# A retuned issue plan for an attention and gated-MLP kernel: new plan table, out-projection gates, earlier tile loads and 24 more dummy matmuls

## The chip, the core and the metric

The kernel runs on one core of a Trainium2 chip. The metric is device time in microseconds (us) of one execution, taken as the median of several runs; lower is better. A profile is one execution of its own, with its own time.

## What is computed

One token block of 2048 x 640 goes through a layernorm without weights. The result `xn` feeds two branches: full softmax attention with 32 heads of 20 columns and an out-projection, and a gated MLP with 1728 hidden columns whose output goes through silu. The two are multiplied and added to the input.

```python
def _A_ref(x, wqkv, wo):                       # x: [1, 2048, 640], H = 32, Dh = 20
    qkv = (x @ wqkv).reshape(B, S, 3, H, Dh).transpose(2, 0, 3, 1, 4)
    q, k, v = qkv[0], qkv[1], qkv[2]
    p = _softmax(jnp.einsum("bhqd,bhkd->bhqk", q, k) * Dh ** -0.5, axis=-1)
    o = jnp.einsum("bhqk,bhkd->bhqd", p, v)
    return o.transpose(0, 2, 1, 3).reshape(B, S, D) @ wo

def _B_ref(x, w_gate, w_up, w_down):           # F = 1728
    h = _sigmoid(x @ w_gate) * (x @ w_up)
    return h @ w_down

xn = _layernorm(A_x)
return A_x + _A_ref(xn, A_wqkv, A_wo) * _silu(_B_ref(xn, B_w_gate, B_w_up, B_w_down))
```

## The kernel before

**Stages.** A prologue (the list `PRO`, written out by hand) loads the 16 token tiles, normalizes and transposes them into `xnT`, and makes the first keys, values and queries. `s_warm` and `s_tr` put dummy 128x128 matmuls (`dummies`, line 318) between its TensorE (PE) steps. `s_k` makes the four key chunks; the maximum of the keys (`s_km`, `s_mdp`, `s_md`) gives a bound that one matmul, `s_bound`, subtracts from the scores of the first query; `s_qe0` moves that query to SBUF. Then the first scores can start.

The main part walks over 32 blocks, each of four heads and 512 queries. A block has 64 score tiles of 128 keys x 512 queries. A score matmul uses 32 rows of the PE array (L928). A score tile is turned into exponentials in one of two ways: ScalarE (ACT) applies Exp (L142, `pt`), or VectorE (DVE) makes it by integer arithmetic: one pass per tile from PSUM (`iv`, L1305) and three passes per group of four tiles in SBUF (`pb`, L1016, L1019, L1022). Both feed the PV matmuls (L964), which use 21 columns of the array; four of them, one for each head, run side by side.

**PSUM.** `scA` is two slots of two banks each, filled by turns. One turn is called a slot here: PE writes two score tiles into `scA`, often a third for ACT or one or two for DVE into the four single banks `bk`; ACT then takes the two-bank tile (128x1024) and, where there is one, the third tile (128x512). PE can only refill a slot when ACT has read it. The four `bk` banks also hold the PV sum of the block, and the results of all other matmuls.

**The other work** is cut into items that fill PE between the scores: key, query and value projections, GLU matmuls (L704, L716), the down projection (L742) with its tanh on ACT, and, late, the out-projection (`mk_out`, matmuls L802; `mk_part`, matmuls L835, for the last 512 queries). An out-projection item has a PE step, then a DVE step `ev`: it multiplies the PSUM tile by the stored MLP output (`otmp`, L809), and POOL (or DVE, at the end) adds the input tile (L812). `load_out` (L778) loads both operands of a token tile, the input rows (L783) and the MLP rows `gq_dram` (L784), into memory that `xnT` no longer needs; two token tiles alternate, so a load waits until the tile two before has been used and stored. It is called when the first half of a tile starts on PE.

**What sets the order.** The order of PE, ACT and DVE is fixed when the program is built: a planner steps a model clock (`now`) in 0.01 us, keeps when each engine, bank and buffer comes free, and writes the next instruction for a free engine. At run time each engine goes through its list in order and waits where an operand isn't ready. The planner's choices depend on eighteen numbers (`RULE`, L38), which are replaced at the start of each block by a row of `PLAN` (L41): how long to hold PE for a score slot, how many tiles DVE may take, how many ready PV tiles open a bank (`held`), and so on. An item opens when its `pre` events are past in the model; a step of it can have `gates` as well. POOL and the DMA queue of SyncE (SP) are not in the planner: a scheduler orders them.

**Normalization.** At the end of a block DVE copies the PV sum (`norm_a`, L978), its row of sums goes through DRAM (`ld`, `lt`), DVE takes the reciprocal `rt` (`norm_b`, L988, in the model 6.5 us after the copy), which goes through DRAM once more (`rd`, `rl`), and POOL multiplies (`norm_c`, L1001). For the last block but one the result `o6` goes straight to SBUF (L1005). The last block uses a short chain on the engines (`chain`, L1080): ACT copies the sum (L1061), PE transposes, DVE divides (`rq`, L772, and `onq`), PE transposes back, ACT copies (L1078), and `tail_steps` closes with the last out-projection matmuls (L1052, L1056), DVE multiplies (L1098, L1105) and adds, and four stores.

Of the kernel before, what the change touches and what calls it, by code (L numbers as in the profile page):

```python
# [18 lines left out]
P = 128  # L19
# [19 lines left out]
            dmax=2, third=2, dord=0, mord=0, mfew=2, npv=4, held=48, burst=1, excl=1)  # L39
KEYS = tuple(RULE)  # L40
PLAN = (  # L41
    (0.25, 5, 0.15, 0.2, 0.5, 0, 0.4, 1, 0.0, 2, 2, 0, 0, 2, 4, 48, 1, 1),
    (0.25, 5, 0.15, 0.2, 0.5, 0, 0.4, 1, 0.0, 2, 1, 0, 3, 2, 4, 48, 1, 1),
    (0.25, 4, 0.15, 0.2, 0.8, 0.2, 0.4, 1, 8.0, 2, 2, 0, 0, 2, 4, 48, 1, 1),
    (0.25, 4, 0.15, 0, 0.8, 0.2, 0.4, 1, 0.0, 2, 2, 0, 0, 2, 4, 48, 0, 1),
    (0.25, 4, 0.15, 0, 0.8, 0.2, 0.4, 1, 0.0, 2, 2, 3, 0, 2, 4, 48, 0, 0),
    (0.2, 4, 0.15, 0.2, 0.2, 0.2, 0.4, 1, 0.0, 2, 2, 0, 0, 1, 4, 32, 1, 1),
    (0.25, 4, 0.15, 0.5, 0.8, 0.2, 0.4, 1, 0.0, 2, 2, 0, 0, 2, 4, 48, 1, 1),
    (0.25, 4, 0.3, 0.2, 0.35, 0.2, 0.4, 1, 0.0, 2, 2, 0, 0, 1, 4, 48, 1, 1),
    (0.25, 4, 0.3, 0.2, 0.35, 0.8, 0.4, 1, 0.0, 2, 2, 0, 0, 1, 4, 48, 1, 1),  # L50
    (0.3, 4, 0.3, 0.2, 0.35, 0.8, 0.4, 1, -2.0, 2, 2, 0, 0, 1, 4, 48, 1, 1),
    (0.3, 4, 0.3, 0.2, 0.35, 0.8, 0.4, 1, -2.0, 2, 2, 0, 0, 1, 4, 48, 1, 1),
    (0.25, 4, 0.15, 0.2, 0.2, 0.2, 0.4, 1, 0.0, 2, 2, 0, 0, 2, 4, 48, 0, 1),
    (0.2, 4, 0.15, 0.2, 0.2, 0.2, 0.2, 1, 0.0, 2, 2, 0, 0, 2, 4, 48, 0, 1),
    (0.25, 4, 0.15, 0.2, 0.2, 0.2, 0.4, 1, 0.0, 2, 0, 0, 0, 1, 4, 48, 0, 1),
    (0.25, 4, 0, 0.2, 0.2, 0.2, 0.4, 1, 0.0, 2, 0, 0, 0, 1, 4, 48, 1, 1),
    (0.25, 4, 0, 0, 0.2, 0.2, 0.4, 1, 4.0, 2, 0, 0, 0, 1, 4, 48, 1, 1),
    (0.3, 4, 0.15, 0.2, 0.2, 0.2, 0.4, 1, 0.0, 2, 2, 0, 0, 2, 4, 48, 1, 1),
    (0.3, 4, 0.15, 0.2, 0.2, 0.5, 0.7, 1, 0.0, 2, 2, 0, 0, 2, 4, 48, 1, 1),
    (0.25, 4, 0.15, 0.2, 0.2, 1.2, 0.4, 1, 0.0, 2, 2, 0, 0, 2, 4, 48, 1, 1),  # L60
    (0.25, 4, 0.15, 0.2, 0, 1.2, 0.4, 1, 0.0, 2, 2, 0, 0, 2, 4, 48, 1, 1),
    (0.25, 4, 0.3, 0.2, 0, 1.2, 0.4, 1, 0.0, 2, 2, 0, 0, 1, 4, 48, 1, 1),
    (0.25, 4, 0.3, 0.2, 0.5, 1.2, 0.4, 1, 0.0, 2, 1, 0, 0, 1, 4, 48, 1, 1),
    (0.25, 4, 0, 0.2, 0.8, 1.2, 0.4, 1, 0.0, 2, 2, 0, 0, 2, 4, 48, 1, 1),
    (0.25, 4, 0.15, 0.2, 0.2, 0.5, 0.4, 1, 0.0, 2, 1, 0, 0, 2, 4, 48, 1, 1),
    (0.45, 4, 0.15, 0.2, 0.2, 0.5, 0.4, 1, 0.0, 2, 1, 2, 0, 2, 4, 52, 1, 1),
    (0.25, 4, 0.15, 0.2, 0.2, 0.2, 0.4, 1, 0.0, 2, 1, 0, 0, 2, 4, 48, 1, 1),
    (0.25, 4, 0.15, 0.2, 0.2, 0.5, 0.4, 1, 0.0, 2, 1, 0, 0, 2, 4, 48, 1, 1),
    (0.25, 4, 0.15, 0.5, 0.2, 1.2, 0.4, 1, 0.0, 2, 2, 0, 2, 2, 4, 48, 1, 1),
    (0.25, 4, 0.15, 0.2, 0.35, 0.2, 0.4, 1, 0.0, 2, 2, 0, 0, 2, 4, 48, 1, 1),  # L70
    (0.25, 4, 0.15, 0.2, 0.2, 0.2, 0.4, 1, 0.0, 2, 0, 0, 0, 2, 4, 48, 1, 1),
    (0.25, 4, 0.15, 0.2, 0.35, 0.8, 0.4, 1, 14.0, 2, 1, 0, 0, 2, 4, 48, 1, 1),
    (0.25, 4, 0.15, 0.2, 0.2, 0.2, 0.4, 1, 0.0, 2, 2, 0, 0, 2, 4, 48, 1, 1),
)

PRO = (
# [35 lines left out]
def kernel(  # L112
# [146 lines left out]
    with tc.tile_pool(name="ln", bufs=2) as lp, \  # L259
# [105 lines left out]
        def s_k(eng, c):  # L365
            pks[c] = psP.tile([P, 512], FP32, tag="pk", bufs=1, name="psk")
            k_mm(pks[c], 0, c)

        def s_km(eng, c):
            maxed.append(c)  # L370
# [29 lines left out]

        def s_bound(eng):
            q_bound(pq[0], 0, pq[1])

        def s_qe0(eng):
            q_evac(pq[0], qts[0])
# [104 lines left out]
    def mk_k(g, c, at):  # L510
        st = {}

        def alloc():
            st["ps"] = misc_ps()
        mms = [lambda kd=kd: k_mm1(st["ps"], g, c, kd) for kd in range(KD)]
        return Item([("PE", alloc, [(T_MM, f) for f in mms]),
                     ("DVE", 0.66, lambda: k_evac(st["ps"], g, c), "free"),
                     ("DVE", 0.60, lambda: k_max(g, c), "", lambda t: mds_done(g, t))], at)

    def mds_done(g, t):  # L520
        if len(mk_n[g]) == NQC:
# [45 lines left out]
    def mk_ku(u, c, at):  # L567
        st = {}

        def alloc():  # L570
            st["ps"] = misc_ps()

        def ev():
            st["k"] = wk.tile([P, QC], BF16, tag="ku", bufs=2, name="ku")[0:UC, :]
            nc.vector.tensor_copy(out=st["k"], in_=st["ps"][0:UC, :])
            nc.sync.dma_start(out=kD[u][:, c * QC:(c + 1) * QC], in_=st["k"])

        def mx():
            if u not in mku:
                mku[u] = [wk.tile([UC, NQC], FP32, tag="mk4", bufs=2, name="mk4"), 0, None]  # L580
            nc.vector.tensor_reduce(out=mku[u][0][:, c:c + 1], in_=st["k"], axis=AXISX, op=ALU.max,
                                    apply_absolute_value=True)
            mku[u][1] += 1
            if mku[u][1] == NQC:
                mk = wk.tile([UC, 1], FP32, tag="mk", bufs=2, name="mk")
                nc.vector.tensor_reduce(out=mk, in_=mku[u][0], axis=AXISX, op=ALU.max)
                mku[u][2] = wk.tile([UC, UH], BF16, tag="mdu", bufs=2, name="mdu")
                nc.vector.tensor_scalar_mul(out=mku[u][2], in0=esum_u[0:UC, :], scalar1=mk[:, 0:1])

        def end(t):  # L590
            if mku[u][1] == NQC:
                ev_at[("mdu", u)] = t + 0.3
        return Item([("PE", alloc, [(T_MM, lambda kd=kd: u_mm(st, u, 1, c, kd)) for kd in range(KD)]),
                     ("DVE", 0.60, ev, "free", mark("kD", u, c)), ("DVE", 0.60, mx, "", end)], at,
                    pre=[("wu", u)])

    aqs = {}
# [180 lines left out]
    def load_out(tt):  # L778
# [3 lines left out]
        out_tiles[tt] = (o2[:, 0:D], o2[:, D:3 * D].bitcast(FP32))  # L782
        nc.sync.dma_start(out=out_tiles[tt][0], in_=x2[tt * P:(tt + 1) * P, :])  # L783
        nc.sync.dma_start(out=out_tiles[tt][1], in_=gq_dram[tt * P:(tt + 1) * P, :])  # L784

    def pool_hold(t):
        pool_from[0] = max(pool_at[0], t)
# [2 lines left out]
    def mk_out(tt, h, at):  # L790
        st = {}

        def alloc():
            if h == 0:
                load_out(tt)
                if tt == 0:
                    load_out(1)
            st["ps"] = misc_ps()

        def mm(kd):  # L800
# [4 lines left out]
        def ev():  # L805
# [7 lines left out]
            if h == 1:  # L813
                nc.sync.dma_start(out=out2[tt * P:(tt + 1) * P, :], in_=xr)
                if tt + 2 < TT - 4 and all(("d", (tt + 2) // 4, t4, i) in ev_at for t4 in range(4) for i in range(2)):
# [1 line left out]
        return Item([("PE", alloc, [(0.136, lambda kd=kd: mm(kd)) for kd in range(KD)]),  # L817
                     ("DVE", 0.40, ev, "free", lambda t: (mark("o", tt, h)(t), pool_hold(t)))], at, need=blk(NG - 1, tt // 4),
                    pre=[("d", tt // 4, t4, i) for t4 in range(4) for i in range(2)] + [("wo",), ("oc", tt // 4)] + (
                        [("o", tt - 2, 1)] if h == 0 and tt > 1 else []))  # L820


    wdf = wd.rearrange("p k e -> p (k e)")[:, 0:8 * D].bitcast(FP32)
# [290 lines left out]
    with tc.manual_schedule(engines={ENG.PE, ENG.Activation, ENG.DVE}):  # L1114
# [64 lines left out]
        while chain or items or glu_items or o_next < NQC or any(it.i < len(it.ops) for it in active):  # L1179
# [10 lines left out]
            if ("wo",) not in ev_at and base() >= PAIR and ("bD", NU - 1) in ev_at and all(  # L1190
                    v_at.get((NG // 2 - 1, t), 1e9) <= now for t in range(TT)) and all(
                    ev_at.get(("h", 2, kf), 1e9) <= now for kf in range(NFT)):
                ev_at[("wo",)] = now + 6.0
                for kd in range(KD):
                    nc.sync.dma_start(out=wo[kd], in_=A_wo[kd * P:(kd + 1) * P, :])
                for i in range(2):
# [35 lines left out]
            for eng in ("ACT", "DVE"):  # L1232
# [7 lines left out]
                    continue  # L1240
                if eng == "DVE" and norm_pending is not None and norm_pending[1] <= now and norm_pending[0] < NBLK - 1:
                    free["DVE"] = now + T_ON
                    timed.append((free["DVE"] + 6.5, norm_pending[0]) + norm_a(norm_pending[0]))
                    flex[pv_bank[0]] = now + T_ON + EL["DVE"]
                    pv_bank[0] = None
                    norm_pending = None
# [269 lines left out]
```

## Time and profile before

| | |
|---|---|
| median of 7 runs (lowest to highest) | 811.72 us (810.55 to 814.33) |
| the profiled execution: time, span of its instructions | 814.33 us, 812.6 us |
| ACT busy | 784.8 us, 97% of the span |
| DVE busy | 774.6 us, 95% |
| PE busy | 774.6 us, 95% |
| POOL busy | 93.3 us, 11% |
| mean granted PE clock | 0.989 of full speed |

The profiled execution is the slowest of the seven. Rows of the same engine can overlap in the trace (an instruction starts while the one before it is finishing), so what an instruction costs its engine is read from the start of one to the start of the next, and idle time is only a part of what is lost. The granted clock of PE is 1.00 or 0.50 in any moment; the clock of a window is the mean over it.

### The profile page before, as it was taken

How to read it: one execution, taken by the hardware profiler on the slowest of the kernel's cores; microseconds unless marked ns; L12 is line 12 of the kernel's file. 1: busy time of each engine (PE TensorE's matmuls, PEld its weight loads, DVE VectorE, ACT ScalarE, POOL GpSimd, SP SyncE). 2: the span in 40 equal slices, each digit the busy share in tenths (PEclk: the TensorE clock that was granted, in tenths of full speed). 3: DMA queues.
4: the chain of work that ended last, by engine and by line, in shares of the span. 5: the costliest groups of instructions: out<-in, count | busy, mean ns of one | idle time of the engine just before them, and what ended most of it. 6: DMA issues, size and time to landing. Idle time of an engine off the chain costs nothing.

```text
span 812.6 us, 17165 instructions
## 1 busy us (share of the span) xinstructions
PE 774.6 (95%) x6490; PEld 274.9 (34%) x6490; DVE 774.6 (95%) x1272; ACT 784.8 (97%) x1003; POOL 93.3 (11%) x107
## 2 busy tenths in 40 slices
PE   6899999999999999999999999999999999899995
PEld 5432333332333333333323223333332223233332
DVE  8799999998999999999999999999999999999996
ACT  8799999998999999999999999999999999999992
POOL 6000000000000000000000000000000001401346
PEclk9999999997999999999999999999999999999998
DMA  5521311122122222321113323143122330510431
GB/s 165 162 57 48 100 48 51 53 59 73 56 72 59 73 68 74 96 62 51 35 55 87 90 81 84 47 128 94 41 86 68 85 91 27 162 51 26 141 122 56
DMA packets 95876, 62.62 MB, mean 77 GB/s; under 512 B 36388, under 2 KB 89684, under 8 KB 95792
## 3 DMA queue, kind: packets, MB, share of 16 engines
q1 hardware_dynamic: 95504, 61.18, 26.7%
q8 instruction: 51, 0.84, 0.4%
q10 hardware_dynamic: 288, 0.33, 0.1%
q14 instruction: 33, 0.27, 0.1%
HBM read 47.84 MB, written 13.55 MB: 76 GB/s over the span
## 4 chain that ended last, share of the span: by engine, by line
ACT 53%; PE 30%; DVE 11%; issue 4%; DMA 1%; SPq 1%; POOL 0%; DVEq 0%; ACTq 0%
ACT pt L142 48%; PE scA L928 10%; PE bk L964 7%; PE bk L742 6%; PE bk L704 3%; DVE iv L1305 3%; ACT tnh L142 3%; DVE pb L1022 1%; PE bk L564 1%; DVE pb L1016 1%; PE bk L802 1%; ACT td L142 1%; DVE pb L1019 1%; DVE hT L712 1%; PE bk L928 0%
## 5 line engine op out<-in xcount | busy, mean ns | idle before, releaser
L142 ACT ACTIVATE pt<-scA 128x1024 bf16<-128x1024 f32 x696 | 715.5, 1234 | 3.7 <-PE bk L928 1.6
L1305 DVE TENSOR_SCALAR iv<-bk 128x512 int16<-128x512 f32 x497 | 332.5, 684 | 13.4 <-PE bk L928 12.0
L928 PE MATMUL scA<-q,kT 32*128 32x512 bf16 x1391 | 272.3, 384 | 15.7 <-ACT pt L142 11.7
L928 PE MATMUL bk<-q,kT 32*128 32x512 bf16 x657 | 206.5, 386 | 0.5 <-DVE otmp L809 0.2
L964 PE MATMUL bk<-pt,v 128*21 128x512 bf16 x1551 | 182.4, 385 | 0.0
L928 PEld LDWEIGHTS <-kT 32*128 32x128 bf16 x2048 | 86.7, 91 | 267.6 <-issue 255.2
L964 PE MATMUL bk<-pb,v 128*21 128x512 bf16 x994 | 157.2, 386 | 0.8 <-DVE pb L1016 0.7
L1022 DVE TENSOR_TENSOR pb<-iv,pb 128x2048 bf16<-128x2048 bf16 (+1 forms) x125 | 152.1, 1217 | 0.4
L704 PE MATMUL bk<-xnT,wgu 128*128 128x512 bf16 x520 | 144.3, 382 | 1.4 <-DVE iv L1305 0.6
L142 ACT ACTIVATE pt<-bk 128x512 bf16<-128x512 f32 x160 | 128.8, 805 | 3.2 <-DVE bk L424 1.7
L1001 POOL TENSOR_TENSOR on_bf<-on,rl 128x512 bf16<-128x512 f32 x31 | 42.4, 1367 | 663.8 <-DVE rl L999 577.7
L1016 DVE TENSOR_SCALAR pb<-iv 128x2048 int16<-128x2048 int16 (+1 forms) x125 | 88.7, 709 | 0.7
L742 PE MATMUL bk<-wd,hT 128*128 128x320 bf16 x448 | 87.5, 306 | 1.2 <-DVE hT L724 1.0
L1019 DVE TENSOR_SCALAR pb<-iv 128x2048 int16<-128x2048 int16 (+1 forms) x125 | 86.3, 691 | 0.1
L964 PEld LDWEIGHTS <-v 128*21 128x21 bf16 x2545 | 47.4, 90 | 87.3 <-issue 70.8
L704 PEld LDWEIGHTS <-wgu 128*128 128x128 bf16 x520 | 39.1, 97 | 64.5 <-issue 41.4
L742 PEld LDWEIGHTS <-hT 128*128 128x128 bf16 x448 | 35.6, 98 | 44.0 <-issue 33.2
L142 ACT ACTIVATE tnh<-bk 128x512 bf16<-128x512 f32 (+1 forms) x56 | 46.2, 825 | 0.1
L564 PE MATMUL bk<-xnT,wu 128*128 128x512 bf16 x160 | 44.4, 382 | 0.0
L712 DVE SCALAR_TENSOR_TENSOR hT<-tnh,bk 128x512 bf16<-128x512 bf16 x52 | 35.6, 685 | 1.2 <-PE bk L704 0.5
L812 POOL TENSOR_TENSOR xnT<-otmp,xnT 128x320 bf16<-128x320 f32 x24 | 24.2, 1026 | 42.6 <-DVE otmp L809 33.6
L672 PE MATMUL bk<-wv,xnT 128*128 128x160 bf16 x280 | 27.1, 239 | 0.2
(116 smaller groups left out, 390.6 us busy)
## 6 DMA issues: line engine op xcount, KB each, us to landing
rl<-rd SPq DMA_DIRECT2D x124, 64.0 KB
wgu<-in_B_w_gate_dram SPq DMA_DIRECT2D x24, 320.0 KB
wgu<-in_B_w_up_dram SPq DMA_DIRECT2D x24, 320.0 KB
gq_dram<-gqs SPq DMA_DIRECT2D x24, 160.0 KB
xnT<-gq_dram SPq DMA_DIRECT2D x12, 320.0 KB
xt<-in_A_x_dram SPq DMA_DIRECT2D x16, 160.0 KB
oD<-on_bf SPq DMA_DIRECT2D x120, 20.0 KB
wd<-in_B_w_down_dram SPq DMA_DIRECT2D x1, 2080.0 KB
```

The source lines that it names most:

```text
L142: return nc.scalar.add_instruction(mybir.InstActivation(func=func, name=nc.get_next_instruction_name(), engine=ENG.Activation, ins=[nc.sca ...
L564: nc.tensor.matmul(st["ps"], lhsT=wus[u][:, kd, i, :], rhs=xnT[:, c, kd, :], start=(kd == 0), stop=(kd == KD - 1))
L704: nc.tensor.matmul(st[key][0:fs, :], lhsT=w[:, i, kd, ko * P:ko * P + fs], rhs=xnT[:, c, kd, :], start=(kd == 0), stop=(kd == KD - 1))
L712: nc.vector.scalar_tensor_tensor(out=hT[0:fs, kf, :], in0=st["t"][0:fs, :], scalar=1.0, in1=st["u"][0:fs, :], op0=ALU.add, op1=ALU.mult)
L742: nc.tensor.matmul(st["ps"][:, 0:HD], lhsT=hT[0:fsz[kf], kf, t4 * P:(t4 + 1) * P], rhs=wd[0:fsz[kf], kf, h * HD:(h + 1) * HD], start=(kf = ...
L928: nc.tensor.matmul(dst, lhsT=kTs[gc(b)[0] % 2][32 * j:32 * j + 32, kt * P:(kt + 1) * P], rhs=qts[b % 3][32 * j:32 * j + 32, :], start=True ...
L964: nc.tensor.matmul(bank[pv_bank[0]][32 * j:32 * j + DH + 1, :], lhsT=lhsT, rhs=u["src"], start=first, stop=last, tile_position=(0, 32 * j) ...
L1001: nc.gpsimd.tensor_tensor(out=on_bf, in0=on, in1=rl, op=ALU.mult)
L1016: nc.vector.tensor_scalar(out=pb[:, 0, :, :].bitcast(I16), in0=iv, scalar1=0x7F80, scalar2=1, op0=ALU.bitwise_and, op1=ALU.bitwise_or)
L1019: nc.vector.tensor_scalar(out=pb[:, 1, :, :].bitcast(I16), in0=iv, scalar1=0x007F, scalar2=0x3F00, op0=ALU.bitwise_and, op1=ALU.bitwise_or)
L1022: nc.vector.tensor_tensor(out=pb[:, 1, :, :], in0=iv.bitcast(BF16), in1=pb[:, 1, :, :], op=ALU.mult)
L1305: nc.vector.tensor_scalar(out=d["iv"][:, j, :], in0=bank[bk], scalar1=B_OFF, scalar2=0.0, op0=ALU.add, op1=ALU.max)
```

## The change

Four things. (1) `s_k` puts 14 dummy matmuls behind the last key chunk, and `s_bound` 10 behind the bound matmul. (2) `load_out(0)` and `load_out(1)` are issued when the out-projection weights are loaded, not when the first item starts; `load_out` sets an event 4.0 us later in the model, and the DVE step of `mk_out` is gated by it. (3) Three model durations change: the last key maximum of a group costs 1.05 instead of 0.60, and the reciprocal comes 7.0 instead of 6.5 us after the copy. (4) All 32 rows of `PLAN` are replaced. A row holds the values of `RULE` in its order; two rows of each are shown.

```diff
 RULE = dict(urgent=0.25, rounds=4, hold=0.15, slack=0.2, s0=0.2, s1=0.2, wait3=0.4, fall=1, lag=0.0,
             dmax=2, third=2, dord=0, mord=0, mfew=2, npv=4, held=48, burst=1, excl=1)
 PLAN = (
-    (0.25, 5, 0.15, 0.2, 0.5, 0, 0.4, 1, 0.0, 2, 2, 0, 0, 2, 4, 48, 1, 1),
...
-    (0.25, 4, 0.15, 0.2, 0.2, 0.2, 0.4, 1, 0.0, 2, 2, 0, 0, 2, 4, 48, 1, 1),
+    (0.25, 4, 0.15, 0.2, 0.2, 0.8, 0.2, 1, 0.0, 2, 2, 0, 0, 1, 4, 48, 1, 1),
...
+    (0.25, 4, 0.15, 0.2, 0.2, 0.8, 0.4, 1, 0.0, 2, 2, 0, 0, 2, 4, 16, 0, 1),
+    (0.25, 4, 0.15, 0.2, 0.2, 0.8, 0.4, 1, 0.0, 2, 2, 0, 0, 2, 4, 16, 0, 1),
 )
...
         def s_k(eng, c):
             pks[c] = psP.tile([P, 512], FP32, tag="pk", bufs=1, name="psk")
             k_mm(pks[c], 0, c)
+            if len(pks) == NQC:
+                warm[0] = psP.tile([P, 2 * P], FP32, tag="tp", bufs=4, name="warm2")
+                dummies(14)
...
         def s_bound(eng):
             q_bound(pq[0], 0, pq[1])
+            dummies(10)
...
-                     ("DVE", 0.60, lambda: k_max(g, c), "", lambda t: mds_done(g, t))], at)
+                     ("DVE", 1.05 if c == NQC - 1 else 0.60, lambda: k_max(g, c), "", lambda t: mds_done(g, t))], at)
...
         nc.sync.dma_start(out=out_tiles[tt][1], in_=gq_dram[tt * P:(tt + 1) * P, :])
+        ev_at[("ol", tt)] = now + 4.0
...
             if h == 0:
                 load_out(tt)
-                if tt == 0:
-                    load_out(1)
...
-                        [("o", tt - 2, 1)] if h == 0 and tt > 1 else []))
+                        [("o", tt - 2, 1)] if h == 0 and tt > 1 else []), gates={1: [("ol", tt)]})
...
                 ev_at[("wo",)] = now + 6.0
+                load_out(0)
+                load_out(1)
...
-                    timed.append((free["DVE"] + 6.5, norm_pending[0]) + norm_a(norm_pending[0]))
+                    timed.append((free["DVE"] + 7.0, norm_pending[0]) + norm_a(norm_pending[0]))
```

The change of `ev` durations for the MLP-side keys (`mk_ku`) is the same as that of `mk_k`. Because every row of `PLAN` is new, the order of nearly all instructions of the main part changes, while the work stays what it was: ACT gets 696 exponentials of 128x1024, 3 of 128x512 from `scA` and 155 of 128x512 from `bk` (before 695, 1 and 160), DVE 498 `iv` tiles (before 497), and one of the 24 adds of L812 moves from POOL to DVE.

## The prediction

> **What bounds the kernel now.** I read the page's engine and clock lines first.
>
> ```profile
> PE 774.6 (95%) x6490; PEld 274.9 (34%) x6490; DVE 774.6 (95%) x1272; ACT 784.8 (97%) x1003; POOL 93.3 (11%) x107
> ...
> ACT  8799999998999999999999999999999999999992
> ...
> PEclk9999999997999999999999999999999999999998
> ```
>
> ACT is the busiest engine, and it is full but for the first and last slices and one near 190 us, the only one in which the clock line falls to 7. What an exponential costs ACT is read from start to start in the timeline:
>
> ```profile
> 641.31 1.29 ACT L142 ACTIVATE pt<-scA 128x1024 bf16<-128x1024 f32 x1
> 642.22 0.87 ACT L142 ACTIVATE pt<-bk 128x512 bf16<-128x512 f32 x1
> 642.69 2.23 ACT L142 ACTIVATE pt<-scA 128x1024 bf16<-128x1024 f32 x2
> ```
>
> 642.22 - 641.31 = 0.91 us for the wide form (0.90 over all such pairs) and 642.69 - 642.22 = 0.47 for the narrow one (0.48 over all). A GLU tanh takes 0.48, a down-projection tanh 0.32. With these, all ACT work from the first exponential (30.2 us) is 746.5 us; measured against it, ACT loses 24.7 us until its last instruction. By stretches of 25 us the loss is 0.3 to 0.6 nearly everywhere; the exceptions are 4.5 at 175 to 200, 1.4 at 675 to 700, 2.1 at 700 to 725 and 5.2 from 775 on. Only these can be won, so ACT's exponentials are the bound and the plan is worth what it does to a few places.
>
> Next the windows around the slow clock, cut at its edges:
>
> ```profile
> 25.97:29.39 3.42, 1.51 (x6) 0.38 (x4) 1.83 (x4) 0.69 (x1) 0.00 (x0) 1.00 0.00 0
> 29.39:32.80 3.41, 3.26 (x23) 2.26 (x24) 1.87 (x3) 2.57 (x4) 0.00 (x0) 0.50 0.94 242
> 186.40:189.81 3.41, 1.93 (x18) 0.86 (x17) 3.32 (x8) 3.36 (x6) 0.00 (x0) 1.00 0.72 188
> 189.81:193.22 3.41, 3.41 (x16) 0.92 (x13) 3.13 (x5) 2.68 (x3) 0.00 (x0) 0.50 0.55 149
> 196.64:200.05 3.41, 3.41 (x29) 0.46 (x21) 1.69 (x4) 2.39 (x3) 0.00 (x0) 0.50 0.00 0
> ```
>
> The first busy number is PE; the one after POOL is the clock. It halves for one window of 3.41 us at 29.39 and for three from 189.81 to 200.05; the two starts are 47 such windows apart, so the chip seems to decide window by window. Each drop follows a thin window.
>
> PE's timeline says why 186.40 was thin:
>
> ```profile
> 188.28 0.39 PE L928 MATMUL scA<-q,kT 32*128 32x512 bf16 x2 [1.27 <-ACT pt L142]
> ```
>
> Three score slots stand behind one another in PE's list, and PE waits 1.27 us for ACT to free the place of the third. The waits (us in all, times, longest) name a part of what costs 675 to 725 and 785:
>
> ```profile
> DVE otmp L809 <- DMA xnT<-gq_dram: 1.5, 2, 0.9
> ```
>
> DVE stands at an out-projection step whose MLP rows haven't landed, with score tiles behind it.
>
> **The change part by part**, against the profiled execution's own 814.33 us (span 812.6 and 1.7 around it). It is the slowest of seven; the median is 2.6 lower.
>
> *Dummies.* Behind the last key chunk PE waits 1.18 us for the bound, then 0.79 for the query. In the warm prologue (9.0 to 10.5) 24 128-column matmuls took 1.5 us, 0.063 each: 14 take 0.88 and 10 take 0.63. Both fit into the waits, so they delay nothing; a wait of half its length would let up to 0.3 us through. They lift the thin window of 25.97 by 1.3 us of matmuls, so the scores start at full clock. ACT's first exponential moves from 30.23 to about 29.9 (a score row is 0.61 long here, 0.39 later), and the 0.5 lost at 32.1 behind slow value matmuls goes: -0.8.
>
> *The drop at 190.* From 189.50 to 200.65 ACT starts eight wide exponentials and needs 8 x 0.90 = 7.2 us of 11.15: 3.9 lost, 4.2 with the waits before it. In the new order no three slots stand behind one another (before: once). -4.2.
>
> *ACT's work.* One wide exponential more, two 128x512 from `scA` more, five narrow fewer: 0.90 + 2 x 0.48 - 5 x 0.48 = -0.5.
>
> *Out-projection gates.* 675 to 725 loses 3.4, of which 0.8 is the usual. The gate keeps the step off DVE's list for 4.0 us after the load is written, but the bank stays taken meanwhile, and the model's time isn't SP's: a load still stands in SP's queue behind the store of the tile before (for tile 10 the store is issued at 783.06, the input load at 785.53, 2.5 later). Between 0 and -2.6; neither end is nearer, I take -1.3, and -0.4 of the 0.8 between 785 and the end of the scores. The early loads of tiles 0 and 1 bring nothing: the first `otmp` at 687.37 waits for no DMA. They put four issues of some 0.35 us ahead of the weights on SP; those have 6 us in the plan.
>
> *The other durations.* The reciprocal 0.5 later spares up to the 1.8 that DVE waits for `lt` in all; DVE isn't the bound: 0.
>
> *The end.* One add moves from POOL to DVE, in front of the chain's reciprocal. It is that of tile 11, whose input load stands behind the four `o6` loads and the store of tile 9. SP's and POOL's timelines of before show such a load and its wait:
>
> ```profile
> 785.01 0.34 SPq L814 DMA_DIRECT2D out_dram<-xnT  x1
> 785.53 0.33 SPq L783 DMA_DIRECT2D xnT<-in_A_x_dram  x1
> ```
>
> ```profile
> 788.60 0.79 POOL L812 TENSOR_TENSOR xnT<-otmp,xnT 128x320 bf16<-128x320 f32 x1 [3.62 <-DMA xnT<-in_A_x_dram]
> ```
>
> Here POOL waited 3.62 for such a load. In the new order `rt` of the last block but one stands some ten slots (13 us) before the last exponential, not 10 us. From `rt`, 2.8 to the broadcast, 1.8 of issue, 1.5 to land, up to 2.3 on POOL, 1.4 to 3.1 for the `o6` issues, 0.35 and 2.5 for the store, 1.1 to land: the input is there 13 to 16 us after `rt`, 0 to 3 after the last exponential; then the add (1.03) and one `otmp` (0.4). The reciprocal came 3.1 after the last exponential before. So -0.6 (the rest of DVE's list is done sooner) to +2.8; +0.3, as the middle of the arrivals still meets 3.1.
>
> *A new thin stretch.* PE's new list, between slots 678 and 685 (of 699; 24 us of ACT work before the last exponential), holds no item of other work at all. By slot: score tiles 3, 3, 3, 3, 4, 3, 3, 3 and PV matmuls 0, 4, 3, 3, 2, 0, 12, 0. ACT needs 0.48 + 4 x 1.38 + 3 x 0.90 = 8.7 us for them, two and a half windows. I weigh windows by the share of the array: five 512-column matmuls in 1.24 us are 0.215 each, and a score or PV matmul uses a quarter of the array, 0.054. Then 186.40 has 10 L928 + 5 L672 (160 columns) + 3 L742 (320) = 0.54 + 0.34 + 0.40 = 1.28 us, 37%, and dropped; 25.97 has 31% and dropped; the thinnest that didn't drop is 415.09, 42%. The new stretch has 49 quarter matmuls, 2.63 us of 8.7, 30%, and any whole window inside it holds 28 to 32%. So the clock falls there, in every execution, some 3.4 to 6.8 us into it. While PE is thin this costs about nothing. From slot 686 on the array is needed 9.2 of 14.6 us, 63%; the slow windows of before did 37, 39 and 39%, so each slow microsecond loses 1 - 0.385/0.63 = 0.39. One window earlier the clock returned after one window of 42% and after a third of 39%. With 3 to 9 us slow behind slot 686, 6 likely: +2.4 (0 to +3.5).
>
> Here a rule speaks the other way. The Trainium skill, "TensorE: Matmul & The Clock Gate", section "Why this matters for your kernels", asks only that no idle gap between matmuls exceed about 3 us. This trace shows a drop whose longest gap was 1.27 us, so the row decides; by the rule the new stretch, with no gap over some 1.1 us, would cost nothing and the sum be 807.4.
>
> Sum: 814.33 - 0.8 - 4.2 - 0.5 - 1.3 - 0.4 + 0.3 + 2.4 = 809.8 us. As the drop at 190 isn't in every execution (814.33 - 4.2 = 810.1, near the lowest run) but the late one should be, I read this as the median too.
>
> **The rivals.** (a) *The late stretch costs nothing*: the clock holds, or returns before slot 686. For it: 708.64 is thin by PE's busy time too (2.42 of 3.41) and held. Against it: the shares. 814.33 - 6.9 = 807.4.
> (b) *Slow to the end*, the slower side: the mix after slot 686 keeps the windows at the 37 to 39% that twice did not bring the clock back. Then 9.2 us of array work go at 38.5%, 23.8 us for 14.6, +9.2, and about 1 in the tail: 809.8 - 2.4 + 10.2 = 817.6. It decides if two windows behind slot 686 fail; from three failed on it is slower than before. Near 190 two failed, so it is no small chance.
> (c) *The end waits for tile 11*: the input lands 3 us after the last exponential and the chain behind it: 809.8 + 2.5 = 812.3.
> (d) *The gates do nothing*, since SP runs behind the model: 809.8 + 1.7 = 811.5.
>
> **How the numbers follow.** About 0.2% (1.6 us) is what a measurement of this kernel can tell from no change, so faster is under 810.1 and slower over 813.3. Forecast 0.40, own range 807.5 to 812; (a) 0.26, 805 to 809.5; (b) 0.20, 813.5 to 819; (c) 0.08; (d) 0.06. Faster: 0.22 of the forecast, all but 0.01 of (a), 0.02 of (c) and (d): 0.49. Slower: 0.20 from (b), 0.03 each from forecast and (c), 0.01 from (d): 0.27. The rest, 0.24, is the same. The range of 805.2 to 815.5 leaves out the upper two thirds of (b) and a little of (a): the lower end is (a) with the gates' whole 2.6 and 0.8.
>
> **What would show it.** In the new profile: clock 1.00 at 29 to 33 and the first exponential before 30.0; no slow window near 190; a slow one about 20 us before the last exponential, with ACT's losses behind it. Wrong if the clock line is full there, if it is slow to the end, if new waits of ACT stand in other stretches, or if DVE's L815 (L812 before) waits for a DMA in front of the reciprocal.

## The result and the profile after

The changed kernel is slower: 814.61 us median (811.12 to 816.73, 26 runs) beside 811.21 for the kernel before (808.36 to 814.33, 64 runs), a ratio of 1.0037 with a 95% interval of 1.0029 to 1.0046. Forecast were 809.8 us in a range of 805.2 to 815.5. The profiled execution took 813.78 us (span 812.1), below the median of its kernel, while the profiled execution of before lay 3.1 above its own. A second profile of before, taken later (run e5 below), took 810.45 us (span 808.8) at the same mean clock as after's, 0.992. It is the better partner, and both are used.

The page of after, with the lines that answer to those shown of before:

```profile
PE 776.5 (96%) x6515; PEld 276.8 (34%) x6515; DVE 774.7 (95%) x1274; ACT 782.4 (96%) x1001; POOL 88.7 (11%) x106
...
ACT  8899999999999999999999999999999999999990
...
PEclk9999999999999999999999999999999999999997
```

The clock line's 7 near 190 us is gone, and with it the 8 at the same place of ACT's line; ACT's second digit is 8 where it was 7. But ACT's last digit is 0 where it was 2: no exponential starts in the last slice (20 us). The exponentials end earlier, and what follows them is longer.

The accounts close like this. The span is: start of the first exponential, ACT's work (all exponentials and tanhs and seven small copies of queries, up to the last exponential), what ACT loses beside it, the last exponential (0.90), and the tail behind it.

| us | before, first profile | before, second | after |
|---|---|---|---|
| first exponential starts | 30.23 | 29.44 | 29.82 |
| work up to the last exponential | 744.6 | 744.6 | 744.1 |
| lost up to there | 20.75 | 17.78 | 16.02 |
| of it 25-50 / 175-200 | 0.53 / 4.54 | 1.11 / 0.57 | 0.12 / 0.78 |
| of it 675-725 / 750-775 / 775 on | 3.44 / 0.37 / 1.19 | 3.22 / 0.35 / 1.62 | 2.89 / 1.28 / 0.14 |
| last exponential starts | 795.60 | 791.84 | 789.93 |
| tail behind its end | 16.10 | 16.01 | 21.25 |

Against the second profile the exponentials end 1.9 us earlier and the tail is 5.2 longer: 3.3 us slower, close to the difference of the medians (3.4).

Two slow windows are left in this execution of after, up to the last 6 us (windows cut at the clock's edges; the first busy number is PE, the number behind POOL's is the clock):

```profile
768.45:771.87 3.42, 1.83 (x15) 0.66 (x15) 3.42 (x6) 3.42 (x6) 0.00 (x0) 1.00 0.17 49
771.87:775.28 3.41, 3.25 (x26) 0.72 (x29) 2.88 (x5) 3.03 (x6) 0.00 (x0) 0.50 0.07 18
...
792.35:795.76 3.41, 1.64 (x11) 1.07 (x12) 1.40 (x4) 0.59 (x1) 2.35 (x3) 1.00 0.32 96
795.76:799.17 3.41, 3.37 (x16) 2.09 (x16) 2.02 (x5) 0.58 (x1) 2.52 (x4) 0.50 0.17 53
```

The first pair is the thin stretch of the prediction: 24% of the array in the window (weighed as there), then one window at half clock. Other executions had more: in the profiles of e4, e8, e13 and e14 below, whose order is the same here, the clock stayed at half for three windows. In e8:

```profile
765.86:769.27 3.41, 1.86 (x18) 0.76 (x19) 3.35 (x5) 3.41 (x6) 0.00 (x0) 1.00 0.09 24
769.27:772.68 3.41, 3.03 (x25) 0.59 (x21) 3.29 (x5) 3.07 (x4) 0.00 (x0) 0.50 0.15 43
772.68:776.10 3.42, 3.14 (x23) 0.63 (x19) 3.00 (x5) 3.34 (x4) 0.00 (x0) 0.50 0.00 0
776.10:779.51 3.41, 3.41 (x20) 0.76 (x18) 2.63 (x6) 2.05 (x2) 0.79 (x1) 0.50 0.03 2
```

The second pair of after lies in the tail. What delays the tail is in the queue of SP, in POOL's and in DVE's timeline of after (start, duration, instruction, the idle time before it and what ended it):

```profile
786.47 3.12 SPq L1008 DMA_DIRECT2D o<-on_bf  x4
789.70 0.42 SPq L787 DMA_DIRECT2D xnT<-in_A_x_dram  x1
790.15 0.43 SPq L817 DMA_DIRECT2D out_dram<-xnT  x1
792.60 0.33 SPq L787 DMA_DIRECT2D xnT<-in_A_x_dram  x1
```

```profile
792.30 1.54 POOL L815 TENSOR_TENSOR xnT<-otmp,xnT 128x320 bf16<-128x320 f32 x2 [5.11 <-DMA xnT<-in_A_x_dram]
794.89 1.10 POOL L815 TENSOR_TENSOR xnT<-otmp,xnT 128x320 bf16<-128x320 f32 x1 [1.06 <-DMA xnT<-in_A_x_dram]
...
799.20 3.97 POOL L846 TENSOR_TENSOR wd<-otmp,xr 128x320 f32<-128x320 f32 x5 [0.75 <-DVE otmp L844]
```

```profile
793.12 0.49 DVE L812 SCALAR_TENSOR_TENSOR otmp<-bk,xnT 128x320 f32<-128x320 f32 x1 [2.38 <-POOL xnT L815]
794.85 0.49 DVE L815 TENSOR_TENSOR xnT<-otmp,xnT 128x320 bf16<-128x320 f32 x1 [1.24 <-DMA xnT<-in_A_x_dram]
```

The input rows of tile 10 (L787 at 789.70) stand behind the four `o6` issues, those of tile 11 (792.60) behind the store of tile 9. POOL waits 5.11 us for the one and 1.06 for the other. DVE waits for POOL, as `otmp` has three buffers (2.38), and then for tile 11's rows itself (1.24). Behind all this stand the eight `mk_part` items of the last 512 queries (before had one of them done when the last exponential ended); the last of their POOL adds (L846) ends at 803.17, and the last of their DVE steps, held back by the same three buffers, at 801.7. Only then can the closing matmuls start. In PE's timeline of after, then of the second profile of before:

```profile
801.75 0.81 PE L1055 MATMUL bk<-wo_t,o 80*128 80x128 bf16 x6 [0.65 <-DVE otmp L844]
```

```profile
798.36 0.92 PE L1052 MATMUL bk<-wo_t,o 80*128 80x128 bf16 x6
```

The last step of the chain, ACT's copy `o`, ends at 798.91 and 797.68 in the two. So before, the closing matmuls start 0.7 us behind the chain; in after the chain has been ready for 2.8 us, and they wait for the parts. From the first closing matmul to the end of the span 10.3 and 10.4 us pass, so the start of these matmuls, 10.9 instead of 5.6 us behind the last exponential, is the whole difference of the tails.

### The profile page after: what moved, and what is told of

It is laid out like the page before. It is cut to its first block, busy times and chain, and to the rows that moved or that the text cites. A ratio compares the mean times of both kernels' runs of the same rounds, so it can differ in the third digit from the quotient of the medians.

```text
span 812.1 us, 17201 instructions
## 1 busy us (share of the span) xinstructions
PE 776.5 (96%) x6515; PEld 276.8 (34%) x6515; DVE 774.7 (95%) x1274; ACT 782.4 (96%) x1001; POOL 88.7 (11%) x106
## 4 chain that ended last, share of the span: by engine, by line
ACT 49%; PE 37%; DVE 7%; issue 4%; DMA 2%; SPq 1%; POOL 0%; DVEq 0%; ACTq 0%; POOLq 0%
ACT pt L142 42%; PE scA L931 12%; PE bk L967 9%; PE bk L708 6%; PE bk L746 5%; DVE iv L1310 3%; ACT tnh L142 2%; PE bk L568 1%; ACT td L142 1%; PE bk L931 1%; DVE pb L1025 1%; ACT sq L338 1%; ACT xnT L362 1%; DVE pb L1022 1%; DVE hT L716 1%
## 5 line engine op out<-in xcount | busy, mean ns | idle before, releaser
L142 ACT ACTIVATE pt<-scA 128x1024 bf16<-128x1024 f32 (+1 forms) x699 | 711.6, 1228 | 1.7 <-PE bk L931 1.5
L1310 DVE TENSOR_SCALAR iv<-bk 128x512 int16<-128x512 f32 x498 | 330.6, 684 | 10.4 <-PE bk L931 8.2
L931 PE MATMUL bk<-q,kT 32*128 32x512 bf16 x653 | 203.1, 385 | 1.0 <-DVE otmp L812 0.9
L967 PE MATMUL bk<-pb,v 128*21 128x512 bf16 x996 | 160.9, 384 | 0.1
L142 ACT ACTIVATE pt<-bk 128x512 bf16<-128x512 f32 x155 | 121.8, 786 | 2.0 <-PE bk L931 1.7
L746 PE MATMUL bk<-wd,hT 128*128 128x320 bf16 x448 | 85.4, 302 | 1.2 <-DVE iv L1310 0.8
L815 POOL TENSOR_TENSOR xnT<-otmp,xnT 128x320 bf16<-128x320 f32 x23 | 21.7, 949 | 60.4 <-DVE otmp L812 51.9
```

Source lines behind the costliest of these rows:

```text
L142: return nc.scalar.add_instruction(mybir.InstActivation(func=func, name=nc.get_next_instruction_name(), engine=ENG.Activation, ins=[nc.sca ...
L746: nc.tensor.matmul(st["ps"][:, 0:HD], lhsT=hT[0:fsz[kf], kf, t4 * P:(t4 + 1) * P], rhs=wd[0:fsz[kf], kf, h * HD:(h + 1) * HD], start=(kf = ...
L931: nc.tensor.matmul(dst, lhsT=kTs[gc(b)[0] % 2][32 * j:32 * j + 32, kt * P:(kt + 1) * P], rhs=qts[b % 3][32 * j:32 * j + 32, :], start=True ...
L967: nc.tensor.matmul(bank[pv_bank[0]][32 * j:32 * j + DH + 1, :], lhsT=lhsT, rhs=u["src"], start=first, stop=last, tile_position=(0, 32 * j) ...
L1310: nc.vector.tensor_scalar(out=d["iv"][:, j, :], in0=bank[bk], scalar1=B_OFF, scalar2=0.0, op0=ALU.add, op1=ALU.max)
```

## The experiments

All ratios are to the kernel before, run beside them on the same chip.

**e3, own memory for the rows of tiles 10 and 11.** Their loads no longer wait for the stores of tiles 8 and 9, nor stand behind `o6`; the order of PE, ACT, DVE and POOL stays.

```diff
-        out_tiles[tt] = (o2[:, 0:D], o2[:, D:3 * D].bitcast(FP32))
-        nc.sync.dma_start(out=out_tiles[tt][0], in_=x2[tt * P:(tt + 1) * P, :])
+        own = {TT - 6: xfl[:, 2 * KD * QC - D:2 * KD * QC], TT - 5: hfl[:, 0:D]}
+        out_tiles[tt] = (own.get(tt, o2[:, 0:D]), o2[:, D:3 * D].bitcast(FP32))
+        if tt not in own:
+            nc.sync.dma_start(out=out_tiles[tt][0], in_=x2[tt * P:(tt + 1) * P, :])
+        for t, at_t in ((TT - 6, TT - 8), (TT - 5, TT - 6)):
+            if tt == at_t:
...
+                nc.sync.dma_start(out=own[t], in_=x2[t * P:(t + 1) * P, :])
```

> The kernel after with memory of their own for the input rows of output tiles 10 and 11, loaded before the stores of tiles 8 and 9 are issued; the issue order of PE, ACT, DVE and POOL is the same as after's. Theory 1 (the tail waits for these two loads: POOL's adds at 792.30 waited 5.11 us, the DVE add at 794.85 waited 1.24): the reciprocal of the last block's chain comes 1.5 to 2.5 us earlier, the eight parts start 3 to 4 us earlier, TensorE has no thin window there, the tail is 16.5 to 18.5 us instead of 21.3: 810 to 812 us against after's 814.6, ratio to before 0.998 to 1.001. Theory 2 (the eight parts behind the last score with their 8 x 0.79 us of GpSimd adds set the tail, whenever the rows land): the tail stays at 20 us or more, 813.5 to 814.6 us, ratio 1.0025 to 1.004.

Measured: 811.84 us, ratio 0.9992 (0.9976 to 1.0008), against 1.0037 for after; the tail is 18.17 instead of 21.25. The reciprocal `rq` now starts 2.9 us after the last exponential's end instead of 4.8. The closing matmuls start 7.8 us behind the last exponential, 2.9 behind the copy `o`. Theory 1 holds for 3.1 of the 5.2 us. What is left of theory 2 is in POOL's timeline of this run:

```profile
796.32 5.27 POOL L852 TENSOR_TENSOR wd<-otmp,xr 128x320 f32<-128x320 f32 x7 [0.75 <-DVE otmp L850]
```

Seven part adds run back to back, 0.75 each, until 801.59.

**e4, the last add of tile 11 back on POOL.**

```diff
-            add = nc.vector if h == 1 and claimed[0] == NJOB * NBLK else nc.gpsimd
-            add.tensor_tensor(out=xr[:, sl], in0=tmp, in1=xr[:, sl], op=ALU.add)
+            nc.gpsimd.tensor_tensor(out=xr[:, sl], in0=tmp, in1=xr[:, sl], op=ALU.add)
```

> The kernel after with the second half's add of tile 11 left on GpSimd (as before the change of order it would have been), so that VectorE never waits for the rows of tile 11 itself. The step as I predicted it (the VectorE add in front of the chain's reciprocal is what costs the end): the reciprocal at 795.66 comes 1 us or more earlier and the time falls by 2 to 4 us, to 810.5-812.5, ratio 0.999 to 1.0015. Theory 1 (the two late loads hold GpSimd, the three-buffer pool and with them VectorE and TensorE, whoever does that add): within 0.8 us of after, 813.8 to 815.4, ratio 1.003 to 1.005.

Measured: 814.03 us, 1.0025 (1.0005 to 1.0045), tail 20.84. Theory 1: the DVE add as such, which the prediction put at the centre of its end term, carries 0.4 us of the tail at most (the slow window in the tail, which this execution doesn't have, is in that 0.4 as well).

**e9, own rows, and three of the eight part adds on DVE.**

```diff
-            nc.gpsimd.tensor_tensor(out=xps[t4][:, sl], in0=tmp, in1=tail[t4][:, sl], op=ALU.add)
+            add = nc.vector if (t4, h) in ((0, 1), (1, 1), (2, 1)) else nc.gpsimd
+            add.tensor_tensor(out=xps[t4][:, sl], in0=tmp, in1=tail[t4][:, sl], op=ALU.add)
```

> The kernel with own memory for the rows of tiles 10 and 11 (ratio 0.9992), and three of the eight 128x320 adds of the last four tiles' parts moved from GpSimd to VectorE. There the eight adds ran back to back on GpSimd from 796.32 for 5.27 us (0.75 each) and VectorE and TensorE waited for them. Theory 2 in its reduced form (with the rows there, GpSimd's adds pace the tail): the tail falls from 18.2 to 16.5-17.2 us: 810 to 811 us, ratio 0.997 to 0.9985. Rival (the chain over on, rq, o7 and the last tiles paces it): no change, ratio 0.999.

Measured: 812.59 us, 1.0010 (0.9993 to 1.0027), tail 19.12. A miss: DVE's timeline of this run shows that two of the three moved adds (0.79 and 0.78) cost what they cost on POOL, and the `otmp` steps stand behind them.

```profile
795.33 0.79 DVE L853 TENSOR_TENSOR wd<-otmp,xr 128x320 f32<-128x320 f32 x1
```

**e15, own rows, and the PLAN rows of the last eight blocks taken from before.**

```diff
 PLAN = (                      # rows 0 to 23 of after
+    (0.45, 4, 0.15, 0.2, 0.2, 0.5, 0.4, 1, 0.0, 2, 1, 2, 0, 2, 4, 52, 1, 1),
...
+    (0.25, 4, 0.15, 0.2, 0.2, 0.2, 0.4, 1, 0.0, 2, 2, 0, 0, 2, 4, 48, 1, 1),
 )                             # rows 24 to 31 of before
```

> Own rows, with the PLAN rows of the last eight blocks taken from before. The order that comes out has two of the eight parts whole and a third begun ahead of the last block's transposes. What is open: whether the 2.0 us by which the tail with own rows (18.2 us from the end of the last exponential) is longer than before's (16.1) is the eight parts behind the last score. If so, the tail falls to 16-17.5 us here and no clock window of 0.5 follows 768-772 us. If the tail is set by the chain through on, rq and o7, it stays at 18 or more. The time up to the last exponential is the order's own and not predicted closely: 809 to 814 us in all, ratio 0.997 to 1.003.

Measured: 811.10 us, 0.9985 (0.9970 to 0.9999); the thin stretch only came some us later (clock 0.50 from 774.33 to 781.16, 2.4 lost from 775 on), and the tail is 18.69. By the expectation a tail of 18 or more speaks for the chain. PE's timeline does not: the chain's copy ended at 797.97, and the closing matmuls still waited for DVE's last part step, which ended at 800.14.

```profile
800.20 0.59 PE L1061 MATMUL bk<-wo_t,o 80*128 80x512 bf16 x2 [0.48 <-DVE otmp L850]
```

So the parts' place in PE's list alone does not decide. Their adds on POOL still came in one run of eight, behind tile 11's, from 795.83 to 801.86. In these five profiles the tail is the end of the last part add plus 8.0 to 9.2 us:

| | last part add ends, after the last exponential's end | the rest of the span | tail |
|---|---|---|---|
| before, second profile | 7.3 | 8.7 | 16.0 |
| own rows (e3) | 9.4 | 8.7 | 18.2 |
| own rows, three adds on DVE (e9) | 9.9 | 9.2 | 19.1 |
| own rows, old late rows (e15) | 10.7 | 8.0 | 18.7 |
| after | 12.3 | 8.9 | 21.3 |

**e12, the clock held by extra matmuls** in the thin stretch and in the tail of after.

```diff
+                            if x < 2 and 1972 <= claimed[0] < 2022:
+                                hold(scA[nfill % 2][:, x, :], t[0], 256 if x else 512)
                             score_mm(scA[nfill % 2][:, x, :] if x < 2 else bank[third], *t)
...
         def alloc():                      # of mk_part
+            if h == 0 and claimed[0] == NJOB * NBLK:
+                hold(scA[1][:, 0, :], NBLK - 1, 512)
+                hold(scA[1][:, 0, :], NBLK - 1, 512)
...
+    def hold(dst, b, n):
+        nc.tensor.matmul(dst[:, 0:n], lhsT=ident, rhs=qts[b % 3][:, 0:n], start=True, stop=True)
```

> The kernel after with about 40 full-array matmuls on dead score banks: 512 and 256 columns ahead of the scores of claims 1972 to 2022 (the thin stretch at 768-772 us, share 24%), and two of 512 columns ahead of every second part of the last tiles (the thin window at 792-796, share 30%). Theory (a window's share of the array's work decides the next window's clock): no slow window at 772 or 796, mean clock of the runs 0.994 instead of 0.991, 1.5 to 3 us less: 811.5 to 813 us, ratio 1.000 to 1.002. Rival (slow windows follow something else, such as TensorE's idle gaps, which stay): clock and time as in after, ratio 1.0035. Rival (the matmuls delay scores by what they save): clock 0.994, time as in after.

Measured: 821.83 us, 1.0134 (1.0110 to 1.0158). The clock did as the theory says (profiled mean 0.996; 1.00 from 768 to 808), but ACT lost 7 us more than in after between 760 and 784, where the holds stood ahead of scores that it waited for; the expected 811.5 to 813 was missed by far: "thin" by PE's count isn't spare time on the path of the scores. The tail was no shorter at full clock (22.0 against 21.3), but here the holds delayed the copy `on` by 3 us, so this run doesn't price the tail's slow window; the idle times of POOL within after's eight adds (0.17 and 0.75) bound it at 0.9.

**e2, all but the PLAN rows**: dummies, gates, early loads, durations.

```diff
 PLAN = (                      # all 32 rows of before, under the rest of the change
```

> Everything of the change but the 32 PLAN rows: dummies, the gate on the landing of the output tiles' rows, the early loads, the longer durations, with the PLAN of before. The issue order that comes out has four half tiles of the out-projection (tiles 10 and 11) and all eight parts of the last four tiles behind the last score, where before has five parts. Theory (the gates are worth little, the tail costs): ScalarE's lost time in 675-725 us falls from 3.4 to 2.2-3.0, and from the end of the last exponential to the end of the span 19 to 23 us pass (before 16.1): 812 to 816 us, ratio 1.001 to 1.006. Rival (the term as I predicted it: gates -1.3 and the tail about +0.3): 809.5 to 810.5, ratio 0.998 to 0.999.

Measured: 830.80 us, 1.0232 (1.0206 to 1.0258), far off either way: the last exponential starts at 800.75 and the tail is 26.6. The old rows don't fit the gated model; the run says that gates and rows are one change, and nothing on the gates' own worth: ACT lost 2.3 us in 675-725, within what was expected, but no less than some runs of the old order without gates lose there (2.5 to 5.6).

**e1 and e6, before with the dummies alone** (the same edit twice).

```diff
             k_mm(pks[c], 0, c)
+            if len(pks) == NQC:
+                warm[0] = psP.tile([P, 2 * P], FP32, tag="tp", bufs=4, name="warm2")
+                dummies(14)
...
             q_bound(pq[0], 0, pq[1])
+            dummies(10)
```

> The kernel before with only the 24 dummy matmuls (14 behind the last K-projection, 10 behind the first row bound). Theory: they keep the clock at 1.00 through 29-33 us, where the profile of before shows 0.50; the first exponential starts near 29.8 us instead of 30.2 and ScalarE's lost time in 25-50 us falls from 0.5 to about 0.1, so 0.4 to 0.8 us in all: ratio to before 0.9990 to 0.9995. Rival: the first exponentials wait for something else too, and the ratio is 1.000.

> The kernel before with only the 24 dummy matmuls, once more, for a second profile and more times. Theory A (they cost something that lasts): 813.5 to 815 us, ratio 1.002 to 1.005, and the profile shows the waits of the first one again (VectorE for the landing of lt at 331 us 2.2 us long, for the store of ku at 427-430, ScalarE's 5.2 us lost in 675-725). Rival B (the first set was chance): ratio 0.999 to 1.001, other waits.

Measured: 814.61 us, 1.0039 (1.0020 to 1.0057), and 815.52, 1.0038 (1.0019 to 1.0057). The clock is 1.00 at 29 to 33 in both and ACT's loss in 25-50 falls to 0.0 as expected. The first exponential does not come earlier: it starts at 30.36 and 30.68, not near 29.8. And both are slower, by 2.8 and 3.9 us. The second profile of before, e5, is the yardstick:

> The kernel before, unchanged: a second profile of it. Theory: the three slow clock windows at 190 us of the first profile (814.33 us, 3 us above the median) are not what a usual execution shows; a profile near the median loses under 1.5 us in 175-200 us and ends its last exponential near 792.5 us instead of 795.6. Ratio 1.000 within 0.0015. Rival: the drop is there again (4 to 5 us lost in 175-200 us), and the change's gain there is a gain against the usual time too.

It came to 811.09 us, 0.9996 (0.9984 to 1.0009), and has no drop at 190 (0.57 lost in 175-200). Held against it, instruction by instruction, e1 falls behind at the same places as e6: 331 us, 423, 427, 693 and 707 to 712. At each of the first two places (331, and 423 to 430 on ACT) 1.0 to 1.2 us go in both runs. The first is DVE's wait for the sums `lt`. In the second profile of before, then in e1:

```profile
329.55 0.25 DVE L988 RECIPROCAL rt<-lt 128x16 f32<-128x16 f32 x1 [1.08 <-DMA lt<-ld]
```

```profile
331.35 0.25 DVE L992 RECIPROCAL rt<-lt 128x16 f32<-128x16 f32 x1 [2.24 <-DMA lt<-ld]
```

The DMA queues of e1 in the 4.35 us before that reciprocal hold one packet that the same stretch of before doesn't (queue, kind, packets, MB, share of 16 engines):

```profile
q1 hardware_dynamic: 2112, 0.58, 57.9%
q8 instruction: 1, 0.02, 1.4%
```

Queue q8 moves 51 packets of 16384 bytes (52 in e10), each 0.9 to 1.9 us long over the profiles, one for about every 256 of PE's 13,000 instructions. The 24 dummies and their weight loads are 48 instructions; they bring every later packet earlier, here from 333.7 (second profile of before) to 329.3 us (328.6 in e6), onto the load of `lt`.

**e7, 24 more dummies in the first stretch instead**, where PE is idle; **e10 and e11, before with 128 and with 64 tiny matmuls** between 50 and 110 us, a whole packet and half of one.

```diff
-            dummies(54)
+            dummies(78)                   # e7
...
     def score_mm(dst, b, kt, j):          # e10: 128; e11: 64
+        if claimed[0] >= 60 and fed[0] < 128:
+            fed[0] += 1
+            nc.tensor.matmul(dst[:, 0:8], lhsT=kTs[gc(b)[0] % 2][32 * j:32 * j + 32, kt * P:(kt + 1) * P],
+                             rhs=qts[b % 3][32 * j:32 * j + 32, 0:8], start=True, stop=True, tile_position=(32 * j, 0))
```

> The kernel before with the same number of dummy matmuls (24) added to the first stretch of 54 at 2.5 us instead, where TensorE is idle until 9.17 us: PE's instruction stream is as much longer, the clock at 29-33 us stays as in before. If the place of the instructions in PE's stream is what makes the dummies slow: 813 to 815, ratio 1.002 to 1.005. If it is the clock or the time of the first exponentials: 811 to 812, ratio 1.000 within 0.0015.

> The kernel before with 128 tiny matmuls (8 columns, a repeat of the score matmul that follows, on the same quarter of the array, output overwritten) between 50 and 110 us, so PE's instruction stream is 256 instructions longer from there: one whole 16384-byte instruction packet. Theory P (where the packets of PE's instructions fall against the waited-for transfers sets 1 to 3 us of the time; 48 more instructions moved one onto lt at 329 us): with a whole packet more, they fall where they fell in before; waits at 331 near 1.1 us, time 811 to 812, ratio 0.9995 to 1.001. Rival (more PE instructions cost, wherever packets fall): 1.002 or more. Rival (the cost of the 24 dummies was the start alone): 1.000 as well, but then the half packet is 1.000 too.

> The same with 64 tiny matmuls: half a packet. Theory P: the packets fall elsewhere than in before, the waits on DMA landings change their places, and the time differs from before's by 0.7 us or more either way; the whole packet does not. Rival (only the number of instructions counts): half of what the whole packet costs.

Measured: e7 813.57 us, 1.0028 (1.0014 to 1.0042), with waits for `lt` of 2.14 and for the store of `ku` of 0.90 at 422, as in e1 and e6; e10 811.59, 0.9997 (0.9983 to 1.0011), `lt` 1.09 and no wait for `ku`, as in before; e11 813.06, 1.0019 (1.0003 to 1.0035), its waits elsewhere (2.1 us for `gq` at 694). ACT falls back by about 1 us at 331 and again at 428 in e7, as in e1 and e6, and by nothing there in e10 and e11. The packet at the second place starts 0.6 to 0.7 us behind the issue of a store of `ku` in e1, e6 and e7 (419.3 to 420.7); in e5, e10 and e11 it starts at 423.3, 423.7 and 415.2, and DVE doesn't wait for the store. So at these two places the extra instructions cost by where they put the packets, not by their number. What e11 loses is not tied to a packet: none lies near 694 (685.6 and 699.5), and its profiled execution, 815.15, is 2.1 above its median, with slow windows near 190 again.

**e8, after without the dummies; e13, e8 with own rows; e14, own rows with 64 tiny matmuls** as in e11.

```diff
-            if len(pks) == NQC:           # e8 and e13; e13 with the edit of e3
-                warm[0] = psP.tile([P, 2 * P], FP32, tag="tp", bufs=4, name="warm2")
-                dummies(14)
...
-            dummies(10)
```

> The kernel after without the 24 dummy matmuls. If they cost about 2.8 us wherever they stand (as beside before): 811 to 812.5 us, ratio to before 0.9995 to 1.0015. If they gain what the prediction gave them (0.4 to 0.8 us): 815 to 815.5, ratio 1.0042 to 1.005.

> The kernel after with own memory for the rows of tiles 10 and 11 and without the 24 dummy matmuls, so that PE's instruction stream is 48 shorter. Theory P (instruction packets): the packet at 688-689 us, on the load of the first output tile's gq (VectorE waited 1.8 us in after, 2.5 in own rows), moves to about 691.7, and that wait falls to 0.5 us as in the run without dummies; the two edits add up: 814.0 less 2.8 to 3.5: 810.5 to 811.5 us, ratio 0.998 to 1.000. Rival (the dummies' clock at 25-34 us is worth more than the packet): 812 to 813, ratio 1.000 to 1.0015.

> Own rows and dummies, with 64 tiny matmuls (8 columns, repeats of the score matmul behind them) between 50 and 110 us: PE's packets come half a packet earlier. Theory P: the packet at 689 moves to about 682 or 696, the wait for gq falls under 1 us, other waits on landings change; the time differs from own rows' 811.8 by 0.5 us or more either way. Rival: no difference from own rows (ratio 0.9992) and the same wait of 2 us at 691.

Measured: e8 814.07 us, 1.0025 (1.0011 to 1.0039), which is neither of the two expected; e13 811.49, 0.9990 (0.9977 to 1.0003); e14 810.94, 0.9982 (0.9967 to 0.9998), the fastest, ahead of after beyond doubt and of before by little. The gate's place shows the packet once more. DVE's timeline of after, then of e8, at the first out-projection tiles:

```profile
691.90 0.49 DVE L812 SCALAR_TENSOR_TENSOR otmp<-bk,xnT 128x320 f32<-128x320 f32 x1 [1.77 <-DMA xnT<-gq_dram]
```

```profile
690.21 0.49 DVE L808 SCALAR_TENSOR_TENSOR otmp<-bk,xnT 128x320 f32<-128x320 f32 x1 [0.50 <-DMA xnT<-gq_dram]
```

With dummies the packet starts at 687.7 to 689.0, while `gq` is loaded, and DVE waits 1.3 to 2.5 us in after, e3, e4 and e9; at 691.7 and 693.6 (e8, e13) it waits 0.5 and 0.4, and in e14 (694.1) no longer for that load. In the whole, dummies out or packets moved are worth 0.3 to 0.9 us in the new order, within the intervals.

## Why the prediction was wrong

Against the profiled execution of before the sum said -4.5 us; measured is -0.5. By its terms:

- *Dummies, -0.8*: in the traced pair -0.8 (the first exponential 0.41 earlier, 0.41 less lost in 25-50). The second half holds: with the dummies 25-50 loses 0 to 0.1 in every profile, without them 0 to 1.4. The first is the pair's luck: the first exponential starts between 29.38 and 30.68 with them and between 29.44 and 30.69 without. And a cost was missing that no row of before showed as such: beside before the kernel became slower by 2.8 and 3.9 us (e1, e6), of which the packets at 331 and 423 to 430 account for some 2.
- *The drop at 190, -4.2*: -3.8 in the traced pair. The median is another matter. In seven profiles of the old order (before, e5, e1, e6, e7, e10, e11) the loss in 175-200 is 4.5, 0.6, 1.9, 0.7, 0.7, 1.8 and 3.2; in the new order 0.8 each time. So the mean gain is 1.1: a usual execution of before had little there to win. The sum doesn't suffer from it. Its base, 814.33, lies 3.1 above the median of before, and 811.21 with a gain of 1.1 and the other terms as they were gives 809.8 again. The error of the sum is elsewhere.
- *ACT's work, -0.5*: -0.5.
- *Gates, -1.3 and -0.4*: -0.55 and -1.05 in the traced pair, together about the size forecast. The wait for `gq` stayed, 1.77 us, as the packet lay on it. Over the profiles 675-725 loses 1.2 to 4.4 in the new order and 2.5 to 5.6 in the old, so one pair doesn't price the gates, and no run here does.
- *The thin stretch, +2.4*: +0.9 in the traced pair, where the clock was back after one window. The drop came where it was forecast in all seven profiles of the new order that keep its late rows and add no holds, but its length differs. In after, e3 and e9 it was one window, beginning 17.7 to 18.3 us before the last exponential. In e4, e8, e13 and e14 it was three, beginning 20.5 to 20.7 us before it, and ACT lost 2.0 us from 775 on instead of 0.1 (after), so the stretch cost about 2.8. The forecast lies between the two; where the windows happen to fall seems to decide. How often each happens in the 27 executions of after is not on record. The share of the array alone is no rule either: the same five matmuls (31% of a window) ahead of 29 us were followed by a drop in before (25.97) and by none in e10 (25.04) and e8 (25.17).
- *The end, +0.3*: +5.2. **This is the step that failed**; its error of 4.9 is larger than that of the whole sum. It asked only how late the add of tile 11 lets the chain's reciprocal run. The rows landed by 794.85, 4.0 us after the last exponential, a little past the forecast's 0 to 3 (`rt` stood 11.8 us ahead of its end, not 13), and the reciprocal came 1.7 us later than before in relation to the last exponential; that much was rival (c). But in the new order the chain doesn't set the end: its copy `o` is ready 2.8 us before the closing matmuls start. The eight parts set it, whose DVE steps and POOL adds the prediction did not follow: POOL stood 5.1 us for the rows of tile 10, and the parts queue behind it. Freeing the rows took 3.1 us away (e3), freeing DVE of the add alone 0.4 (e4). The other 2 us go with the parts' steps on DVE and their adds on POOL, all eight of them behind the last exponential; a kernel in which these come early was not found, so for that share the cause is read from the timelines and the table of tails and not shown by removing it.

The rule of the Trainium skill that the prediction weighed ("TensorE: Matmul & The Clock Gate", "Why this matters for your kernels") again fell short: the drop at 771.87 came although no gap in the window before was longer than 0.7 us. The rival that the clock stays slow to the end did not happen in any profile.

Two of the prediction's sums do not come out. The times listed from `rt` to the landing of the rows add up to 11.5 to 15.5 us, not 13 to 16 (measured: 15.8 in after). And the lower end of the range, (a) with the gates' whole 2.6 and 0.8, is 807.4 - 1.3 - 0.4 = 805.7, not 805.2. Neither changes the account.

## What to carry to other kernels

Follow a late load through every queue that waits for it, and the engine with the many small steps behind it first: here the end was set by eight small steps on VectorE and GpSimd, not by the chain that the eye goes to. Take a second profile before a drop that only one shows is booked as a gain: the drop at 190 was worth 4.2 us in one execution and 1.1 on the mean. The same holds for a cost: the slow clock in the thin stretch took 0.9 us in one profile and about 2.8 in another. And a change that only adds instructions moves what comes after it: on differences under 0.5%, run a variant that shifts the instruction stream alone, before a gain or a loss is put down to the edit.

## What was not expected of the hardware

PE's instructions come in packets of 16384 bytes, one for about every 256 instructions, each 0.9 to 1.9 us long. A packet that falls on a load lengthened the wait for it by 1.0 to 2.0 us (`lt` 1.1 to 2.1-2.4, `gq` 0.5 to 1.3-2.5), and 48 idle instructions at 2.5 us changed a kernel of 811 us by 0.28%, while 256 changed nothing measurable.

The time of a run goes with its mean clock: over the 27 runs of after by 0.63 us per 0.001 (correlation -0.87), over the runs of before beside the experiments by 0.52 (-0.86). A slow window of 3.41 us is 3.41 x 0.5 / 812 = 0.0021 of the mean clock, so about 1.1 to 1.3 us, more than the 0.9 that the term of the window at 771.87 cost. The number of slow windows differs from one execution to the next, and the mean clock with it; most of the spread within these two kernels goes with it.

A 128x320 add from f32 took 0.49 us on DVE while POOL was idle (e9 at 794.00) and 0.79 where POOL had begun one 0.36 us earlier (e9 at 795.33), no faster than on POOL (0.75 to 0.79). Where DVE began first, by 0.04 us, DVE's took 0.49 and POOL's 1.10 (after at 794.85).
